# Attention's products a head at a time in halves of TensorE's rows, state and outputs in two banks

## The chip, the core and the metric

The program runs on one core of one Trainium2 chip. The metric is the device time in microseconds (us) of one execution; the median of several runs counts. Engines are named as in the profile: PE is TensorE, PEld its weight loads, DVE VectorE, ACT ScalarE, POOL GpSimd, SP SyncE. SBUF is the on-chip memory, PSUM the eight banks into which PE writes and from which DVE and ACT read.

## The reference

Three blocks follow each other; the change touches the first. Attention (4 batches, 8 heads, 768 positions, head size 48) is a recurrence with a 48x48 state per head:

```
k_n = k / (norm(k) + 1e-06)
for t in range(768):
    y[t] = q[t] @ state
    state += beta[t] * outer(k_n[t], v[t] - k_n[t] @ state)
```

Then `x = y` as [4, 768, 384] goes through a Fourier mix (a DFT over positions and channels, its real part added), a layer norm and a two-layer MLP of width 1536, and last through a gated block with a mix over positions.

## The kernel before

Attention is done in chunks of 64 positions: 12 chunks a batch, 48 in all, ordered so that the four batches run with a lag of four chunks (`SEQ`). A chunk holds 8 heads as 4 pairs (`HP = 4`): head 0 of a pair lies in partitions 0 to 63, head 1 in 64 to 127. For each chunk the recurrence becomes a 64x64 triangular system, which DVE solves for eight chunks at a time (`solve`, L308 and L313 are its products and sums; 1/8 of a solve is dealt to each step), and a few matrix products on PE, all fp32. An fp32 product is two passes, so four products show as x8.

To keep the two heads of a pair apart, a product before the change takes both in one 128-row pass with zeros in the blocks where the heads would mix:

- `stage_b`: TT (block diagonal, 128x128) times keys and values (128x96), into bank Y. ACT copies each half to WU at columns shifted by head, so that the zeros of WU stand where the other head's columns are (L409, two copies of 64x384).
- `stage_c`, not for a batch's first chunk: WU (112 columns) with the masked products (112 columns) into bank Y; DVE subtracts from qt and leaves cw (L421).
- `stage_d`: for each pair gak (112 columns: 64 of outputs, 48 of the state's change) with WU's values (96 columns), plus cw with the state Sb (the second only when the batch has a state), into one tile pd of bank Y, outputs in partitions 0 to 63, state in 64 to 111. ACT copies the state to the two diagonal blocks of Sb (L446) and the outputs to x (L450). In the last chunk of a batch there is no new state.
- At a batch's seventh chunk (`HALF`) one extra row (L439, xr L441) is taken from the state.

The loop over steps t from -3 to 47 writes the order out by hand: `values(t+2)` (ACT scales values by norms, L397, from chunk 29 on partly DVE), part of the solve on DVE, `stage_d(t)`, `stage_c(t+1)`, `stage_a(t+20)` for the later chunks (t from 4 to 27; L221, 112x128 with zero blocks; it stays), `stage_b(t+2)`, and at odd steps `merge`, which puts the solved 32x32 blocks together in small products (L373, L375) and fills TT (L380; `diag`, L361). `chain` holds every engine to the order in which its instructions were written. Stages A of the first chunks (`pairs0` L186, and L219) already take a head at a time, 48 rows and 64 columns each.

From t = 37 on, steps also take pieces of the DFT of finished batches (L603 to L682) and conversions of MLP weights (L712 to L725). Attention's end runs into the MLP's first products (L829) at about 277 us; from 288 us on PE runs the MLP and the gated block.

PSUM: during attention the banks are shared out as X = 4, Y = 3, Z = 1; pb, pc and pd of stages B, C and D take the banks of Y, each waiting for the release of the one it takes.

Of the kernel before, what the change touches and what calls it, by code (L numbers as in the profile page):

```python
# [7 lines left out]
F32 = mybir.dt.float32  # L8
# [8 lines left out]
B, H, S, D = 4, 8, 768, 48  # L17
# [3 lines left out]
C = 64  # L21
NC = S // C
HP = H // 2
# [42 lines left out]
class Kernel:  # L66
# [51 lines left out]
    def attention(self, cp, pg, pe, p, x, filler, after_solves):  # L118
        nc, a, load = self.nc, self.a, self.load
# [9 lines left out]
        TT = [cp.tile([128, 8, 128], F32, name=f"TT{i}") for i in range(NTT)]  # L129

        WU = [cp.tile([128, HP, 256], F32, name=f"WU{i}") for i in range(NWU)]
        Sb = [cp.tile([112, HP, 96], F32, name=f"Sb{i}") for i in range(B)]
        gas, Tts, st, kqs, qts, preps, seen_a = {}, {}, {}, {}, {}, {}, [0]


# [216 lines left out]
        lo, up = qs[::2], qs[1::2]  # L352


        light = lambda t: t >= 8 * NB - 11

        def diag(g8):

            o = (g8 % 4) * 8
            for us in up:  # L360
                (nc.vector.tensor_copy if light(2 * g8 - 3) else nc.scalar.copy)(out=TT[g8 % NTT][us, :, us], in_=Tts[g8 // 4][us, o : o + 8])  # L361

        def merge(g8, first, second):

            z0, z1 = zz[:, g8 % 2 * 256 : g8 % 2 * 256 + 256].rearrange("p (g n) -> p g n", g=8), zz.rearrange("p (g n) -> p g n", g=8)
            T0, o0 = (Tts[g8 // 4] if first else None), (g8 % 4) * 8
            T1, o1 = (Tts[(g8 - 1) // 4] if second else None), ((g8 - 1) % 4) * 8
            tt = TT[(g8 - 1) % NTT]
            for g in range(8):
                for h in range(2):  # L370
                    if first:
                        ga = gas[g8 * 2 + g // 4][:, g % 4]
                        nc.tensor.matmul(z0[lo[h], g], lhsT=ga[up[h], C : C + 32], rhs=T0[up[h], o0 + g], start=True, stop=True)  # L373
                    if second:
                        nc.tensor.matmul(z1[up[h], g], lhsT=T1[lo[h], o1 + g], rhs=ZS[(g8 - 1) % 2][lo[h], g], start=True, stop=True)  # L375
            if first:
                nc.scalar.mul(ZS[g8 % 2][:96, :, 32:], z0[:96], -1.0)
            if second:
                for h in range(2):
                    nc.scalar.copy(out=tt[lo[h], :, 64 * h : 64 * h + 64], in_=z1[up[h]])  # L380


        def load_kv(bc):
# [15 lines left out]
        def stage_b(bc):  # L399
            kv = gas[bc][:, :, C:]  # L400
            tt, o = TT[(bc // 2) % NTT], (bc % 2) * 4
            pb = self.bank("pb", [128, HP, 2, D])
            for hp in range(HP):
                nc.tensor.matmul(pb[:, hp].rearrange("p t d -> p (t d)"), lhsT=tt[:, o + hp], rhs=kv[:, hp], start=True, stop=True)  # L404
            wu = WU[bc % NWU]
            for h in range(2):
                hs, w = slice(64 * h, 64 * h + 64), 112 - 16 * h
                o_ = wu[hs, :, 64 * h : 64 * h + 2 * w].rearrange("p h (t d) -> p h t d", t=2)[:, :, :, :D]
                nc.scalar.copy(out=o_, in_=pb[hs])  # L409
            st[bc] = [wu[:, :, :112], wu[:, :, 112:208], None]  # L410

        def stage_c(bc):
            qt = qts.pop(bc)
            if SEQ[bc][1] == 0:
                return
            w = st[bc][0]
            cw = p.tile([112, HP, 112], F32, name="cw", bufs=2)
            pc = self.bank("pc", [112, HP, 112])
            for hp in range(HP):
                nc.tensor.matmul(pc[:, hp], lhsT=w[:, hp], rhs=gas[bc][:, hp, : C + D], start=True, stop=True)  # L420
            nc.vector.tensor_sub(cw, qt, pc)  # L421
            st[bc][2] = cw

        def stage_d(bc):
            b, c = SEQ[bc]
            ak = gas[bc][:, :, : C + D]
            w, u, cw = st.pop(bc)
            sb = Sb[b]

            m = 112 if c < NC - 1 else C  # L430
            pd = self.bank("pd", [112, HP, 96])
            for hp in range(HP):
                nc.tensor.matmul(pd[:m, hp], lhsT=ak[:, hp, :m], rhs=u[:, hp], start=True, stop=(c == 0))  # L433
                if c > 0:
                    nc.tensor.matmul(pd[:m, hp], lhsT=cw[:, hp, :m], rhs=sb[:, hp], start=False, stop=True)  # L435
            if c == HALF:
                px = self.bank("pb", [128, HP, 2, D])
                for hp in range(HP):
                    nc.tensor.matmul(px[:1, hp], lhsT=qx[:, b, hp : hp + 1], rhs=sb[:, hp], start=True, stop=True)  # L439
                xr = p.tile([1, DM], F32, name="xr", bufs=2)  # L440
                nc.scalar.copy(out=xr, in_=px[:1].rearrange("p h t d -> p (h t d)"))  # L441
                st["x", b] = xr
            if c < NC - 1:
                for h in range(2):
                    hs, cs = slice(64 * h, 64 * h + 48), slice(48 * h, 48 * h + 48)
# [39 lines left out]
        def busy(n, cols):  # L485
# [33 lines left out]
        for t in range(T0, NBC):  # L519
            j, i = divmod(t + 11, 8)  # L520
# [16 lines left out]
            if t >= 0:  # L537
                stage_d(t)
                if SEQ[t][1] == NC - 1:
                    fill.extend(filler(SEQ[t][0]))  # L540
            new = t % 8 == 5 and t + 3 < NBC
            if new:

                merge((t + 3) // 2, True, False)
                load_kv(t + 3)
                load_kv(t + 4)
                diag((t + 3) // 2)
            if 0 <= t + 1 < NBC:
                stage_c(t + 1)
# [799 lines left out]
```

## Time and profile before

| | us |
|---|---|
| median of 3 runs | 855.77 (855.62 to 856.37) |
| the profiled execution's own time | 856.33 |
| its span, first to last instruction | 854.5 |
| PE busy | 829.6 |
| DVE busy | 623.3 |
| ACT busy | 436.0 |

The span is what the profile's rows lie in; the execution's time has 1.8 us around it. Busy time is the union of an engine's instructions. Matmuls are pipelined and their ends modelled: a pass shows some 0.26 us although the next starts 0.1 us later, so the time that a group of passes takes is read from one group's start to the next one's.

### The profile page before, as it was taken

The numbers are of one execution on the slowest core, as the hardware profiler recorded it, in microseconds if no ns is written. First come the engines' busy times: TensorE is split into PE (matmuls) and PEld (weight loads), VectorE is DVE, ScalarE is ACT, GpSimd is POOL, SyncE is SP. The second block draws the span as 40 slices with busy tenths as digits, with TensorE's granted clock in tenths as the row PEclk, the third lists the DMA queues.
The fourth block names the chain that finished last, engine by engine and source line by source line (L and its number), as shares of the span: only waits on it lengthen the run. The fifth ranks groups of instructions, "written<-read, shape, count | busy, mean of one in ns | idle before, by whom it ended". The sixth has DMA issues, their size and how long they took to land.

```text
span 854.5 us, 18425 instructions
## 1 busy us (share of the span) xinstructions
PE 829.6 (97%) x7117; PEld 803.3 (94%) x7117; DVE 623.3 (73%) x1852; ACT 436.0 (51%) x1054; POOL 7.5 (1%) x29
## 2 busy tenths in 40 slices
PE   7879999999999999999999999999999999999998
PEld 7769999999998999899999999999999899899998
DVE  6989999998969897783654891526688377486563
ACT  2669888788876644232224451223472362543632
POOL 2000000000000000000000000000000000000000
PEclk8869999999999999999999999999999999999999
DMA  9365565556450600001022411122101201101101
GB/s 224 84 178 142 169 187 168 162 160 179 133 145 20 240 1 1 1 1 28 2 71 79 130 31 27 35 59 57 37 1 46 67 9 46 58 18 57 38 1 56
DMA packets 57929, 67.21 MB, mean 79 GB/s; under 512 B 31857, under 2 KB 48978, under 8 KB 57842
## 3 DMA queue, kind: packets, MB, share of 16 engines
q1 hardware_dynamic: 57698, 65.89, 26.8%
q8 instruction: 56, 0.92, 0.5%
q14 instruction: 31, 0.25, 0.1%
q10 hardware_dynamic: 144, 0.15, 0.1%
HBM read 53.62 MB, written 4.72 MB: 68 GB/s over the span
## 4 chain that ended last, share of the span: by engine, by line
PE 87%; DVE 9%; ACT 3%; issue 1%; POOL 0%; DVEq 0%; ACTq 0%; POOLq 0%
PE bankX L829 17%; PE bankY L842 15%; PE bankX L1027 10%; PE bankX L1007 6%; PE bankX L975 6%; PE bankY L1055 5%; PE bankY L433 4%; PE bankY L435 4%; PE bankY L420 4%; PE bankY L404 4%; PE bankX L221 2%; PE bankZ L375 2%; PE bankV L842 2%; PE bankX L642 2%; DVE tm L308 1%; DVE Ts L313 1%
## 5 line engine op out<-in xcount | busy, mean ns | idle before, releaser
L842 PE MATMUL bankY<-w,hx 128*128 128x384 f32 x756 | 147.2, 337 | 0.0
L829 PE MATMUL bankX<-uh,w 128*128 128x384 f32 x504 | 137.7, 340 | 0.7 <-DVE ul L751 0.7
L842 PEld LDWEIGHTS bankY<-w,hx 128*128 128x128 f32 x756 | 132.4, 188 | 0.5 <-issue 0.3
L834 DVE SCALAR_TENSOR_TENSOR hx<-bankX,hx 128x384 fp32r<-128x384 f32 x84 | 46.2, 551 | 76.1 <-ACT hx L833 73.6
L833 ACT ACTIVATE hx<-bankX 128x384 fp32r<-128x384 f32 x84 | 41.2, 490 | 111.9 <-PE bankX L829 107.3
L829 PEld LDWEIGHTS bankX<-uh,w 128*128 128x128 f32 x504 | 92.1, 188 | 1.3 <-DVE ul L751 0.9
L1027 PE MATMUL bankX<-w,A 128*128 128x384 f32 x504 | 88.8, 334 | 0.0
L1027 PEld LDWEIGHTS bankX<-w,A 128*128 128x128 f32 x504 | 87.6, 188 | 0.0
L829 PE MATMUL bankX<-ul,w 128*128 128x384 f32 x252 | 85.1, 338 | 0.0
L433 PE MATMUL bankY<-WU,gak 128*112 128x96 f32 (+1 forms) x384 | 70.2, 271 | 0.7 <-ACT x L450 0.7
L435 PE MATMUL bankY<-Sb,cw 112*112 112x96 f32 (+1 forms) x352 | 64.2, 265 | 3.3 <-DVE cw L421 3.1
L313 DVE TENSOR_TENSOR Ts<-Ts,tm 128x110 f32<-128x110 f32 (+26 forms) x264 | 58.9, 259 | 0.9
L308 DVE TENSOR_TENSOR tm<-Ts 128x110 f32<-128x110 f32 (+26 forms) x264 | 58.5, 258 | 0.4
L404 PE MATMUL bankY<-gak,TT 128*128 128x96 f32 x384 | 52.1, 281 | 4.1 <-ACT gak L397 3.6
L409 ACT COPY WU<-bankY 64x384 f32<-64x384 f32 x96 | 45.4, 473 | 20.5 <-PE bankY L404 18.9
L433 PEld LDWEIGHTS bankY<-WU,gak 128*112 128x112 f32 (+1 forms) x384 | 52.3, 178 | 3.7 <-ACT x L450 1.0
L404 PEld LDWEIGHTS bankY<-gak,TT 128*128 128x128 f32 x384 | 48.7, 199 | 4.9 <-ACT gak L397 4.1
L435 PEld LDWEIGHTS bankY<-Sb,cw 112*112 112x112 f32 (+1 forms) x352 | 48.4, 176 | 4.7 <-issue 2.5
L1007 PE MATMUL bankX<-xh,s 128*128 128x384 f32 x192 | 50.0, 338 | 0.0
L1016 ACT CAST u<-hx 128x384 fp32r<-128x384 f32 x32 | 15.8, 514 | 66.6 <-DVE hx L1014 66.6
L829 PEld LDWEIGHTS bankX<-ul,w 128*128 128x128 f32 x252 | 47.3, 188 | 0.0
L975 PE MATMUL bankX<-s,xh 128*128 128x512 f32 x144 | 45.9, 395 | 0.0
(217 smaller groups left out, 1675.8 us busy)
## 6 DMA issues: line engine op xcount, KB each, us to landing
kq<-in_kq_dram SPq DMA_DIRECT2D x24, 448.0 KB, 4.0
qt<-in_qt_dram SPq DMA_DIRECT2D x48, 196.0 KB, 3.6
gak<-in_kv_dram SPq DMA_DIRECT2D x48, 192.0 KB, 3.9
w<-in_w_dram SPq DMA_DIRECT2D x24, 384.0 KB, 5.6
out_dram<-x SPq DMA_DIRECT2D x24, 192.0 KB, 1.9
kq<-in_kc_dram SPq DMA_DIRECT2D x8, 448.0 KB, 10.8
x<-x SPq DMA_DIRECT2D x96, 36.0 KB, 1.9
s<-in_wi_dram SPq DMA_DIRECT2D x6, 512.0 KB, 4.2
```

The source lines that it names most:

```text
L308: nc.vector.tensor_tensor(out=tm, in0=T[:, r, k : k + 1].to_broadcast(sh), in1=T[:, k : k + 1, :k].to_broadcast(sh), op=MUL)
L313: nc.vector.tensor_add(o, o, tm)
L404: nc.tensor.matmul(pb[:, hp].rearrange("p t d -> p (t d)"), lhsT=tt[:, o + hp], rhs=kv[:, hp], start=True, stop=True)
L409: nc.scalar.copy(out=o_, in_=pb[hs])
L433: nc.tensor.matmul(pd[:m, hp], lhsT=ak[:, hp, :m], rhs=u[:, hp], start=True, stop=(c == 0))
L435: nc.tensor.matmul(pd[:m, hp], lhsT=cw[:, hp, :m], rhs=sb[:, hp], start=False, stop=True)
L829: nc.tensor.matmul(ph, lhsT=w1[f][i][:, c * 128 : c * 128 + 128], rhs=cur[k][:, c], start=(c + j == 0), stop=(c == 2 and j == 2))
L834: nc.vector.scalar_tensor_tensor(out=hl, in0=ph, scalar=0.0, in1=hh.bitcast(F32), op0=MAX, op1=SUB)
L842: nc.tensor.matmul(acc[t], lhsT=hx[i][:, t * 128 : t * 128 + 128], rhs=w2[e][k], start=(e == 0 and j == 0), stop=(e == 11 and j == 2),)
L975: nc.tensor.matmul(pv, lhsT=xT[t][i][:, c, kk * 128 : kk * 128 + 128], rhs=wi[2 * c + 1][k], start=(c + j == 0), stop=(c == 2 and j == 2))
L1007: nc.tensor.matmul(pu, lhsT=wi[2 * c][i][:, f * 128 : f * 128 + 128], rhs=xT[hf][k][:, c], start=(c + j == 0), stop=(c == 2 and j == 2))
L1027: nc.tensor.matmul(acc, lhsT=A[:, m, o, i, kk], rhs=Bo[name, kk][:, k], start=(kk + j == 0), stop=(kk == 2 and j == 2))
```

## The change

Every product of stages B, C and D is taken for one head at a time, with that head's 64 (or 48) rows as the only rows of the pass, and the zero blocks go: TT is 64 columns wide, WU 96, Sb 48. `hs` are the two heads' halves of 64 partitions, `ds` their first 48.

- `stage_b`: 8 products of 64 rows, 64 columns, 96 streamed; one copy of 128x384 to WU.
- `stage_c`: 8 products of 64 rows, 64 columns (48 that count), 112 streamed.
- `stage_d`: state and outputs become products of their own, in two tiles `ps` and `po`, each in its own bank of Y: for each pair, each source (values, state) and each head one product for the state (48 columns) and one for the outputs (64), 48 streamed. Head 0 writes its state to partitions 0 to 47 and its outputs to 64 to 127; head 1 its state to 64 to 111 and its outputs to 0 to 63. The outputs are copied by two instructions of 64x192.
- The extra row: 8 products into partitions 0 and 64, two copies.
- The fills of WU and Sb with zeros go; the fill of TT, whose first tile also feeds the warming products at the start, is half as long.

```
-            for hp in range(HP):
-                nc.tensor.matmul(pb[:, hp].rearrange(...), lhsT=tt[:, o + hp], rhs=kv[:, hp], start=True, stop=True)
+            for hp in range(HP):
+                for h in hs:
+                    nc.tensor.matmul(pb[h, hp].rearrange(...), lhsT=tt[h, o + hp], rhs=kv[h, hp], start=True, stop=True)
...
-            for h in range(2):
-                ...
-                nc.scalar.copy(out=o_, in_=pb[hs])
+            nc.scalar.copy(out=wu, in_=pb.rearrange("p h t d -> p h (t d)"))
...
-                nc.tensor.matmul(pc[:, hp], lhsT=w[:, hp], rhs=gas[bc][:, hp, : C + D], start=True, stop=True)
+                for h in hs:
+                    nc.tensor.matmul(pc[h, hp], lhsT=w[h, hp, :C], rhs=gas[bc][h, hp, : C + D], start=True, stop=True)
...
-            pd = self.bank("pd", [112, HP, 96])
+            po, ps = self.bank("pd", [128, HP, D]), None
+            if c < NC - 1:
+                ps = self.bank("pd", [128, HP, D])
             for hp in range(HP):
-                nc.tensor.matmul(pd[:m, hp], lhsT=ak[:, hp, :m], rhs=u[:, hp], start=True, stop=(c == 0))
-                if c > 0:
-                    nc.tensor.matmul(pd[:m, hp], lhsT=cw[:, hp, :m], rhs=sb[:, hp], start=False, stop=True)
+                for last in (False, True)[: 1 + (c > 0)]:
+                    end = last == (c > 0)
+                    for i, h in enumerate(hs):
+                        k, u = (cw[ds[i], hp], sb[ds[i], hp]) if last else (ak[h, hp], wu[h, hp, D:])
+                        if ps is not None:
+                            nc.tensor.matmul(ps[ds[i], hp], lhsT=k[:, C:], rhs=u, start=not last, stop=end)
+                        nc.tensor.matmul(po[hs[1 - i], hp], lhsT=k[:, :C], rhs=u, start=not last, stop=end)
...
+                for i in range(2):
+                    for hp in range(HP):
+                        nc.tensor.matmul(px[C * i : C * i + 1, hp, i], lhsT=qx[ds[i], b, hp : hp + 1], rhs=sb[ds[i], hp], start=True, stop=True)
+                    nc.scalar.copy(out=xr.rearrange(...)[:, :, i], in_=px[C * i : C * i + 1, :, i])
...
-                    nc.scalar.copy(out=sb[hs, :, cs], in_=pd[64:112, :, cs])
+                for d in ds:
+                    nc.scalar.copy(out=sb[d], in_=ps[d])
...
-            nc.scalar.copy(out=x[b][js, tl], in_=pd[:64].rearrange("p h e -> p (h e)"))
+            for i in range(2):
+                nc.scalar.copy(out=x[b][js, tl].rearrange(...)[:, :, i], in_=po[hs[1 - i]])
...
-        for t in WU + Sb:
-            nc.gpsimd.memset(t, 0.0)
```

## Rows read from the trace of the kernel before

**Rows 1.** The page's part 1: busy us of each engine, share of the span, instructions

```profile
PE 829.6 (97%) x7117; PEld 803.3 (94%) x7117; DVE 623.3 (73%) x1852; ACT 436.0 (51%) x1054; POOL 7.5 (1%) x29
```

**Rows 2.** Windows: stretch; length, then busy PE, PEld, DVE, ACT, POOL (count), granted clock, DMA

```profile
12.00:38.00 26.00, 20.18 (x345) 19.04 (x341) 25.36 (x127) 15.07 (x53) 0.15 (x1) 0.87 0.57 143
38.00:74.00 36.00, 27.94 (x398) 26.32 (x399) 33.21 (x139) 24.81 (x68) 0.82 (x6) 0.72 0.55 142
74.00:190.00 116.00, 115.04 (x1695) 110.39 (x1695) 113.20 (x448) 101.10 (x281) 1.14 (x8) 1.00 0.61 172
190.00:240.00 50.00, 49.45 (x811) 47.16 (x809) 46.47 (x138) 41.16 (x104) 0.15 (x1) 1.00 0.57 160
240.00:288.00 48.00, 46.22 (x476) 43.17 (x474) 37.88 (x98) 33.96 (x79) 0.00 (x0) 1.00 0.38 125
```

**Rows 3.** Timeline of DVE, two stretches: start, us from first start to last end

```profile
27.64 0.46 DVE L308 TENSOR_TENSOR tm<-Ts 128x119 f32<-128x119 f32 x2
...
96.41 0.47 DVE L308 TENSOR_TENSOR tm<-Ts 128x119 f32<-128x119 f32 x2
```

**Rows 4.** Waits from 74 to 240 us: total us, times, longest

```profile
DVE cw L421 <- PE bankY L420: 2.2, 6, 0.6
...
DVE gak L227 <- PE bankX L221: 0.9, 4, 0.3
```

**Rows 5.** Timeline of PE, one step: start, us to the last end, passes (x)

```profile
97.03 0.36 PE L433 MATMUL bankY<-WU,gak 128*112 128x96 f32 x2
...
98.60 0.96 PE L420 MATMUL bankY<-gak,WU 128*112 128x112 f32 x8
99.41 1.07 PE L221 MATMUL bankX<-kq 112*128 112x128 f32 x8
100.31 1.03 PE L404 MATMUL bankY<-gak,TT 128*128 128x96 f32 x8
101.27 0.21 PE L373 MATMUL bankZ<-Tc,gak 32*32 32x32 f32 x1
```

**Rows 6.** Timeline of PEld and PE: loads in halves; products of the last chunk

```profile
8.12 1.36 PEld L186 LDWEIGHTS bankX<-gak 48*64 48x64 f32 x44
...
22.31 1.11 PEld L219 LDWEIGHTS bankX<-kq 48*64 48x64 f32 x19
...
211.31 0.33 PE L435 MATMUL bankY<-Sb,cw 112*64 112x96 f32 x2
211.48 0.33 PE L433 MATMUL bankY<-WU,gak 128*64 128x96 f32 x2
```

**Rows 7.** Timeline of PE around the extra row of a batch

```profile
203.76 0.36 PE L435 MATMUL bankY<-Sb,cw 112*112 112x96 f32 x2
204.05 0.82 PE L439 MATMUL bankY<-Sb,qx 112*1 112x96 f32 x8
204.80 1.04 PE L420 MATMUL bankY<-gak,WU 128*112 128x112 f32 x8
205.67 0.60 PE L404 MATMUL bankY<-gak,TT 128*128 128x96 f32 x4
```

**Rows 8.** Timeline of DVE, late in attention; in brackets the wait before

```profile
254.40 0.56 DVE L725 TENSOR_TENSOR w<-cvd,w 128x384 fp32r<-128x384 f32 x1 [4.54 <-ACT w L724]
```

**Rows 9.** Timeline of ACT in one step

```profile
134.02 0.64 ACT L446 COPY Sb<-bankY 48x192 f32<-48x192 f32 x2
134.67 0.47 ACT L450 COPY x<-bankY 64x384 f32<-64x384 f32 x1
...
136.01 0.97 ACT L409 COPY WU<-bankY 64x384 f32<-64x384 f32 x2
```

**Rows 10.** Timeline of PE, ACT and DVE at another extra row

```profile
94.38 1.04 PE L420 MATMUL bankY<-gak,WU 128*112 128x112 f32 x8
94.65 0.47 ACT L441 COPY xr<-bankY 1x384 f32<-1x384 f32 x1
...
95.88 0.61 DVE L421 TENSOR_TENSOR cw<-qt,bankY 112x448 f32<-112x448 f32 x1
```

More of the change, by code (lines that the diff above doesn't have):

```diff
@@ L128, in attention @@
         NTT = NWU = 2
-        TT = [cp.tile([128, 8, 128], F32, name=f"TT{i}") for i in range(NTT)]
-        WU = [cp.tile([128, HP, 256], F32, name=f"WU{i}") for i in range(NWU)]
-        Sb = [cp.tile([112, HP, 96], F32, name=f"Sb{i}") for i in range(B)]
+        TT = [cp.tile([128, 8, C], F32, name=f"TT{i}") for i in range(NTT)]
+        WU = [cp.tile([128, HP, 2 * D], F32, name=f"WU{i}") for i in range(NWU)]
+        Sb = [cp.tile([112, HP, D], F32, name=f"Sb{i}") for i in range(B)]
+        hs, ds = (slice(0, C), slice(C, 2 * C)), (slice(0, D), slice(C, C + D))
         gas, Tts, st, kqs, qts, preps, seen_a = {}, {}, {}, {}, {}, {}, [0]
@@ L360, in diag @@
             for us in up:
-                (nc.vector.tensor_copy if light(2 * g8 - 3) else nc.scalar.copy)(out=TT[g8 % NTT][us, :, us], in_=Tts[g8 // 4][us, o : o + 8])
+                (nc.vector.tensor_copy if light(2 * g8 - 3) else nc.scalar.copy)(out=TT[g8 % NTT][us, :, 32:], in_=Tts[g8 // 4][us, o : o + 8])
         def merge(g8, first, second):
@@ L379, in merge @@
                 for h in range(2):
-                    nc.scalar.copy(out=tt[lo[h], :, 64 * h : 64 * h + 64], in_=z1[up[h]])
+                    nc.scalar.copy(out=tt[lo[h]], in_=z1[up[h]])
         def load_kv(bc):
@@ L403, in stage_b @@
             for hp in range(HP):
-                nc.tensor.matmul(pb[:, hp].rearrange("p t d -> p (t d)"), lhsT=tt[:, o + hp], rhs=kv[:, hp], start=True, stop=True)
+                for h in hs:
+                    nc.tensor.matmul(pb[h, hp].rearrange("p t d -> p (t d)"), lhsT=tt[h, o + hp], rhs=kv[h, hp], start=True, stop=True)
             wu = WU[bc % NWU]
-            for h in range(2):
-                hs, w = slice(64 * h, 64 * h + 64), 112 - 16 * h
-                o_ = wu[hs, :, 64 * h : 64 * h + 2 * w].rearrange("p h (t d) -> p h t d", t=2)[:, :, :, :D]
-                nc.scalar.copy(out=o_, in_=pb[hs])
-            st[bc] = [wu[:, :, :112], wu[:, :, 112:208], None]
+            nc.scalar.copy(out=wu, in_=pb.rearrange("p h t d -> p h (t d)"))
+            st[bc] = [wu, None]
         def stage_c(bc):
@@ L417, in stage_c @@
             cw = p.tile([112, HP, 112], F32, name="cw", bufs=2)
-            pc = self.bank("pc", [112, HP, 112])
+            pc = self.bank("pc", [128, HP, 112])
             for hp in range(HP):
-                nc.tensor.matmul(pc[:, hp], lhsT=w[:, hp], rhs=gas[bc][:, hp, : C + D], start=True, stop=True)
-            nc.vector.tensor_sub(cw, qt, pc)
-            st[bc][2] = cw
+                for h in hs:
+                    nc.tensor.matmul(pc[h, hp], lhsT=w[h, hp, :C], rhs=gas[bc][h, hp, : C + D], start=True, stop=True)
+            nc.vector.tensor_sub(cw, qt, pc[:112])
+            st[bc][1] = cw
         def stage_d(bc):
@@ L426, in stage_d @@
             ak = gas[bc][:, :, : C + D]
-            w, u, cw = st.pop(bc)
+            wu, cw = st.pop(bc)
             sb = Sb[b]
-            m = 112 if c < NC - 1 else C
-            pd = self.bank("pd", [112, HP, 96])
+            po, ps = self.bank("pd", [128, HP, D]), None
+            if c < NC - 1:
+                ps = self.bank("pd", [128, HP, D])
             for hp in range(HP):
-                nc.tensor.matmul(pd[:m, hp], lhsT=ak[:, hp, :m], rhs=u[:, hp], start=True, stop=(c == 0))
-                if c > 0:
-                    nc.tensor.matmul(pd[:m, hp], lhsT=cw[:, hp, :m], rhs=sb[:, hp], start=False, stop=True)
+                for last in (False, True)[: 1 + (c > 0)]:
[5 more added lines that the diff above has]
+                        nc.tensor.matmul(po[hs[1 - i], hp], lhsT=k[:, :C], rhs=u, start=not last, stop=end)
             if c == HALF:
                 px = self.bank("pb", [128, HP, 2, D])
-                for hp in range(HP):
-                    nc.tensor.matmul(px[:1, hp], lhsT=qx[:, b, hp : hp + 1], rhs=sb[:, hp], start=True, stop=True)
                 xr = p.tile([1, DM], F32, name="xr", bufs=2)
-                nc.scalar.copy(out=xr, in_=px[:1].rearrange("p h t d -> p (h t d)"))
+                for i in range(2):
+                    for hp in range(HP):
+                        nc.tensor.matmul(px[C * i : C * i + 1, hp, i], lhsT=qx[ds[i], b, hp : hp + 1], rhs=sb[ds[i], hp], start=True, stop=True)
+                    nc.scalar.copy(out=xr.rearrange("p (h t d) -> p h t d", h=HP, t=2)[:, :, i], in_=px[C * i : C * i + 1, :, i])
                 st["x", b] = xr
             if c < NC - 1:
-                for h in range(2):
-                    hs, cs = slice(64 * h, 64 * h + 48), slice(48 * h, 48 * h + 48)
-                    nc.scalar.copy(out=sb[hs, :, cs], in_=pd[64:112, :, cs])
+                for d in ds:
+                    nc.scalar.copy(out=sb[d], in_=ps[d])
             cc = c if c < HALF else NC - 1 - c
@@ L449, in stage_d @@
             tl = cc // 2 + (0 if c < HALF else 3)
-            nc.scalar.copy(out=x[b][js, tl], in_=pd[:64].rearrange("p h e -> p (h e)"))
+            for i in range(2):
+                nc.scalar.copy(out=x[b][js, tl].rearrange("p (h t d) -> p h t d", h=HP, t=2)[:, :, i], in_=po[hs[1 - i]])
             if c == NC - 1:
```

## Prediction

> **What bounds the kernel now.** I read the page's busy line first [rows 1]: PE is busy 97% of the span, but its ends are modelled, so the line does not say that a shorter product shortens the kernel. The change lies in attention, which runs to about 288 us, so the second view is the windows by stage [rows 2]. From 74 to 190 us PE is busy 115.04 us of 116 and DVE 113.20; from 190 to 240 us it is 49.45 and 46.47 of 50; only from 240 to 288 us does DVE fall behind, 37.88 of 48 against 46.22. Two engines look full in the loop; one only keeps pace. The third view settles which: DVE's own rows [rows 3]. At 27.64 us, while nothing but the solve of the first block runs, two solver products of 119 columns take 0.46 us. At 96.41 us, in the loop, the same two take 0.47. DVE works at its own pace in the loop, with hardly a hole between instructions. The view of waits agrees: from 74 to 240 us DVE waits for PE's products 2.2 and 0.9 us [rows 4], 3.1 us in 166. So up to 240 us the kernel is bound by DVE, which the change does not touch (the subtraction at L421 keeps its 112x448 shape), and a faster PE can give back some 3 us there, no more. Behind 288 us nothing changes; what attention gains or loses moves the end by as much.
>
> **PE, by products.** An fp32 product is two passes in the rows (x8 for four). Now, with the full array [rows 5]: the 16 passes of stage D (L433, L435) take 98.60 - 97.03 = 1.57 us, 98 ns each with 112 columns of weights; stage C (L420) 0.81; stage A (L221, 128 columns) 0.90, 112 ns each; stage B (L404), also 128 columns, the same 0.90 (0.96 here, with a change of shape behind it, below). With 64 columns of weights and 96 streamed a pass takes 0.17/2 = 85 ns (L435 to L433 at 211 us [rows 6]). In halves of the rows the trace has two kinds: 44 loads of 64 columns within 1.36 us (L186, 64 streamed), at most 31 ns each, and 19 within 1.11 us (L219, 128 streamed), at most 58 [rows 6]. Two halves therefore run beside each other: a pair costs about what one full pass of that shape costs.
> B: 16 passes at 85/2 = 0.68, saving 0.22. C: 16 with 112 streamed, between 85/2 and 58, say 49: 0.79, saving 0.02. D grows from 16 to 64 passes, with 48 or 64 columns of weights and 48 streamed, over all four quarters of the array. The halves in the trace differ in rows and in columns; two passes in the same rows and other columns it does not show. If the quarters run side by side, each has 16 passes at no more than 62 ns (two of L186's 31): 0.99, at best 0.93; D saves 0.6. If only rows overlap, each half has 16 passes at 62 and 16 at some 3/4 of that (48 columns): 1.74, at best 1.6; D loses up to 0.17. No overlap at all is excluded [rows 6]. I take the first, since any two successive blocks of D differ in quarter, which is what L186's passes do, and keep the second for the range.
> [...]
> **A cost that the diff does not name** is the change between array shapes. The row of a batch's extra product shows one [rows 7]: L435 to L439 (one column of weights) 0.29 us instead of 0.20, L439 to L420 0.75 instead of its own eight passes at 80 ns (its 0.82 us less the 0.26 that a single pass shows, over seven), and then L420 0.87 instead of 0.81. That is 0.09 + 0.11 + 0.06, about 0.25 us a round trip. Stage A keeps its full-array products at steps 4 to 27 and now stands between C and B in halves: 24 round trips that were not there. The filler products of the DFT (four steps from 240 us) get one each. The last chunk of a batch, now 64 columns wide in all its products [rows 6], loses its own.
> Sum for PE, per step with A: -0.60 - 0.22 - 0.02 + 0.25 = -0.59 with quarters, +0.18 (up to) with rows alone; without A -0.84 and -0.07.
>
> **What of it reaches the end.** 74 to 240 us: of the 3.1 us of waits I count 2.5 back; the rest of the PE time is hidden by DVE. 240 to 259 us: three steps in which PE sets the pace and DVE stands 4.54 us at once [rows 8]. Two of them gain 0.84 less a round trip and the wait for a bank (below), 0.35 each; the third has a last chunk, whose D is 16 passes of 85 ns and now only outputs, 8 passes of 62 a quarter, 0.9 less. Together 1.6. From 259 us DVE is busy again and I count nothing.
> **ACT**: stage B's two copies (0.97 us the pair [rows 9]) become one of the same 384 columns, 0.48 less; the output copy of 0.47 becomes two of 192 columns, 0.64 by the pair of state copies: +0.17. Net 0.3 less a step on an engine with room (101.10 of 116 [rows 2]): nothing by itself. Should ACT have no room, it is what frees the banks.
> **Banks.** A step took three banks of Y (D, C, B) out of three; now it takes four. B(t+2) can start only when the first of outputs, state and C's bank is free, and that is the state's, after its two copies, 0.64 us behind D's end. C and A (1.7 us) cover it to step 27. Without A, C alone (0.79) does not quite: 0.1 to 0.3 us of PE in some 20 steps. DVE hides most in the loop; I take 0.5 us (bounds 0 and 3).
> **The extra row of each batch** (L439, four times) takes a fifth tile. C must then wait until xr's two copies are done. At 94 us [rows 10] the copy starts at 94.65, behind the values, and takes 0.47; C starts already at 94.38. Two copies of half the length, bounded by 0.47 each and taken as 0.3, put C at 95.25, its end and the subtraction at about 96.2 instead of 95.88: 0.35 us of DVE, more where DVE already waits; three in the loop, 1.5 us (bounds 0.5 and 3).
> **Start.** Fills of WU and Sb go (POOL, off the path: they follow TT's) and TT's halve. TT's fill gates the warming products, so the first real ones may come some tenths earlier: 0.2 us.
> Sum: -0.2 - 2.5 - 1.6 + 0.5 + 1.5 = -2.3 us. The profiled execution took 856.33 us with a span of 854.5 and 1.8 around it: 854.0. It lies 0.56 above the median of the runs shown, so against the median it is 853.5.
>
> **Rivals.**
> *Rows overlap, columns do not* (slower). PE then needs up to 0.18 us more in each of 24 steps with A, 3 to 4 us in all, and since it is now level with DVE [rows 2] it becomes the bound. Without A its saving is 0.07, so that the waits for a bank show: 2.5 us. With the extra rows' 1.5, and 0.5 back between 240 and 259 us, +6: 862. For it: nothing in the trace shows the other. Against it: the passes that do overlap are as short as these. [...]
> *The bank binds* (slower). If B is given the outputs' bank instead of the state's, ACT's chain from values over state and output copies stands ahead of every B. That is 0.64 us later in each step, which A covers no longer once D is short, since ACT's copies, not PE, then set the step. It decides from the point where ACT's work and its waits for B exceed the 4.8 us that a step takes (116 us over 24 steps [rows 2]). At 0.15 us in 24 steps and 0.5 in 10, with 1.5 for the extra rows and 1.6 won back, +8: 864.
> *DVE hides all of it*: what comes back in the loop is less than 1.5 us, the extra rows eat it: 854.5 to 857. This is the upper part of my own case and shares its chance.
> [...]
>
> **How the numbers follow.** A measurement here tells about 0.2% (1.7 us) from no change. Quarters side by side with DVE as bound: 0.55, its own range 850 to 857; over half of it lies beyond 0.2% faster. Rows alone 0.25, the bank 0.10, the earlier clock 0.10. Faster 0.30 + 0.09 = 0.39; same 0.22 from the first and 0.06 from the edges of the others; slower 0.03 + 0.22 + 0.08 = 0.33. The range leaves out a tenth on the slow side and less on the fast one: 848 to 864.
>
> **What would show it.** Right: in the profile after, D of 64 passes in 0.9 to 1.05 us, B in 0.7, A followed and preceded by 0.1 us more; DVE's busy time from 74 to 240 us unchanged and its waits for L420 below 1 us except at the extra rows; the whole loop shorter by under 3 us. Wrong: D at 1.6 us or more; B waiting for ACT's copies of state or outputs for microseconds in sum; a granted clock below 1.00 inside the loop, as PE now has holes there.

## The result, and the profile after

The changed kernel takes 861.9 us (median of 5 runs, 859.28 to 865.49); the kernel before took 856.37 beside it. The ratio is 1.0064, 95% interval 1.0034 to 1.0093: slower by 0.64%, where 853.5 us and faster were forecast. The profiled execution of the changed kernel took 860.85 us, with a span of 859.1.

The page's part 1 (as [rows 1]) and, of part 3, the queue that brings instructions (packets, MB, share):

```profile
PE 803.4 (94%) x9965; PEld 764.4 (89%) x9965; DVE 623.9 (73%) x1852; ACT 419.1 (49%) x1058; POOL 3.5 (0%) x23
...
q8 instruction: 78, 1.28, 0.6%
```

PE is 26 us less busy, DVE does the same work, and yet the span is 4.6 us longer. PE runs 9965 passes instead of 7117, each with a load. The instruction queue had 56 packets before: 22 more packets for 2 x 2848 more instructions, 259 to a packet of 16 KB.

The windows of attention, in the columns of [rows 2], and the last three stretches of half clock within it:

```profile
74.00:190.00 116.00, 102.89 (x3042) 90.84 (x3040) 110.86 (x444) 90.66 (x276) 0.47 (x3) 0.99 0.62 171
190.00:240.00 50.00, 40.79 (x1534) 35.81 (x1528) 46.00 (x137) 36.80 (x104) 0.16 (x1) 1.00 0.57 164
240.00:288.00 48.00, 41.49 (x920) 37.96 (x921) 35.47 (x92) 29.14 (x75) 0.00 (x0) 0.93 0.29 86
...
95.30:98.60 3.30, 3.30 (x77) 3.08 (x79) 3.20 (x16) 1.25 (x4) 0.00 (x0) 0.50 0.42 130
242.10:245.40 3.30, 3.30 (x86) 3.16 (x87) 1.48 (x4) 3.18 (x8) 0.00 (x0) 0.50 0.43 100
276.20:279.50 3.30, 3.30 (x75) 3.02 (x66) 2.62 (x9) 1.16 (x4) 0.00 (x0) 0.50 0.00 0
```

From 74 to 190 us PE fell from 115.04 to 102.89 us, as the shorter products should make it; but DVE, which should have become the only bound, fell too, from 113.20 to 110.86. It waits more. Three times the granted clock drops to half (0.50 in these rows, for 3.4 us each), which it never did behind 63 us before. The waits from 74 to 240 us, PE's and DVE's (as [rows 4]; "issue" is a wait for nothing that the profile shows):

```profile
PE bankY L405 <- ACT Sb L451: 6.9, 11, 1.0
PE bankY L440 <- DVE cw L421: 4.3, 8, 0.8
PE bankY L420 <- issue: 2.0, 2, 1.0
PE bankY L446 <- ACT xr L447: 1.9, 3, 1.0
PE bankY L420 <- ACT xr L447: 1.2, 3, 0.4
PE bankZ L373 <- issue: 1.2, 3, 0.7
...
DVE cw L421 <- PE bankY L420: 4.3, 5, 1.4
DVE gak L227 <- PE bankX L221: 1.6, 4, 0.5
```

DVE's waits for PE went from 3.1 to 5.9 us instead of towards 0.6. PE's waits for cw (4.3 us) are what a PE ahead of DVE must have. Beside them three new waits stand in its list: stage B for the state's copies, the extra row and C for xr's copies, and "issue". When they cost something is seen at the subtraction L421, of which each chunk but a batch's first has one. Its start in the kernel before (us), and how much later (+) or earlier it came in the changed kernel and in four of the runs below:

| start before | changed | row in X | + four banks | fewer instructions | B, C alone |
|---|---|---|---|---|---|
| 58.15 | -0.84 | -1.09 | -0.83 | -0.96 | -1.43 |
| 90.25 | -2.09 | -2.32 | -2.08 | +1.08 | -0.48 |
| 95.88, extra row | -1.14 | -2.32 | -2.08 | +1.08 | -0.44 |
| 115.91 | -0.03 | -2.64 | -2.41 | +0.86 | +1.05 |
| 148.77, extra row | +0.54 | -2.99 | -2.22 | +0.49 | +1.73 |
| 169.16 | +0.47 | -3.34 | -2.29 | +0.24 | +2.22 |
| 174.12 | +1.33 | -1.98 | -1.47 | +0.24 | +2.59 |
| 201.70 | +0.23 | -1.51 | -1.00 | +1.12 | +2.79 |
| 205.87, extra row | +1.13 | -1.65 | -0.99 | +0.69 | +2.67 |
| 210.32 | +1.26 | -0.39 | +1.24 | +0.79 | +2.56 |
| 238.28 | +0.96 | -0.70 | +0.98 | +0.50 | +2.32 |
| 242.39 | +2.83 | -0.71 | +0.98 | +0.50 | +2.50 |
| 248.99, extra row | +3.68 | +0.81 | +1.33 | +1.40 | +2.46 |
| 258.98 | +3.46 | +0.57 | +0.41 | +1.31 | +2.16 |
| 274.84 | +4.13 | +0.64 | +0.93 | +1.38 | +2.38 |

The changed kernel comes 2.1 us early into the loop and loses 6.2 us in it, in jumps: at the four extra rows (0.95, 0.5, 0.9, 0.85), behind the clock's fall at 95 us (1.1), at 174, and at 242.

### The profile page after: what moved, and what is told of

It reads as the page before. It is cut to its first block, busy times and chain, and to the rows that moved or that the text cites. A ratio compares the mean times of both kernels' runs of the same rounds, so it can differ in the third digit from the quotient of the medians.

```text
span 859.1 us, 24110 instructions
## 1 busy us (share of the span) xinstructions
PE 803.4 (94%) x9965; PEld 764.4 (89%) x9965; DVE 623.9 (73%) x1852; ACT 419.1 (49%) x1058; POOL 3.5 (0%) x23
## 4 chain that ended last, share of the span: by engine, by line
PE 77%; DVE 15%; ACT 5%; issue 2%; POOL 0%; DVEq 0%; ACTq 0%; POOLq 0%
PE bankX L832 17%; PE bankY L845 15%; PE bankX L1030 10%; PE bankX L1010 6%; PE bankX L978 6%; PE bankY L1058 5%; DVE tm L308 3%; DVE Ts L313 3%; PE bankY L420 3%; PE bankY L405 2%; PE bankV L845 2%; PE bankX L221 2%; PE bankX L645 2%; PE bankZ L375 2%; PE bankY L440 1%
## 5 line engine op out<-in xcount | busy, mean ns | idle before, releaser
L405 PE MATMUL bankY<-gak,TT 64*64 64x96 f32 x768 | 44.6, 257 | 17.3 <-ACT Sb L451 10.6
L440 PE MATMUL bankY<-WU,gak 64*64 64x48 f32 x768 | 51.3, 231 | 6.8 <-DVE cw L421 5.1
L405 PEld LDWEIGHTS bankY<-gak,TT 64*64 64x64 f32 x768 | 35.8, 139 | 24.5 <-ACT Sb L451 15.0
L420 PE MATMUL bankY<-gak,WU 64*64 64x112 f32 x704 | 47.8, 271 | 4.3 <-issue 2.0
L440 PE MATMUL bankY<-Sb,cw 48*64 48x48 f32 x704 | 47.0, 226 | 1.6 <-issue 0.8
L440 PEld LDWEIGHTS bankY<-WU,gak 64*64 64x64 f32 x768 | 40.5, 141 | 8.7 <-DVE cw L421 6.1
L439 PE MATMUL bankY<-WU,gak 64*48 64x48 f32 x704 | 44.1, 218 | 0.0
```

The lines of the kernel that those rows point to most:

```text
L405: nc.tensor.matmul(pb[h, hp].rearrange("p t d -> p (t d)"), lhsT=tt[h, o + hp], rhs=kv[h, hp], start=True, stop=True)
L420: nc.tensor.matmul(pc[h, hp], lhsT=w[h, hp, :C], rhs=gas[bc][h, hp, : C + D], start=True, stop=True)
L439: nc.tensor.matmul(ps[ds[i], hp], lhsT=k[:, C:], rhs=u, start=not last, stop=end)
L440: nc.tensor.matmul(po[hs[1 - i], hp], lhsT=k[:, :C], rhs=u, start=not last, stop=end)
```

## The experiments

Eighteen kernels tell four causes apart that these jumps suggest: the extra row, the state's bank, the clock, and PE's waits for nothing. All results, with the packets of the instruction queue, PE's "issue" waits from 66 to 290 us, and the median over the runs of the mean granted clock (before: 56, none, 0.984):

| run | us | ratio to before (95%) | packets | issue, us | clock |
|---|---|---|---|---|---|
| changed | 861.9 | 1.0064 (1.0034 to 1.0093) | 78 | 6.7 | 0.978 |
| row in X | 858.8 | 1.0023 (1.0010 to 1.0037) | 78 | 5.8 | 0.981 |
| four banks | 860.3 | 1.0039 (1.0020 to 1.0057) | 78 | 10.3 | 0.982 |
| row in X, four banks | 856.7 | 0.9997 (0.9985 to 1.0010) | 78 | 11.4 | 0.982 |
| row in X, fewer instructions | 853.3 | 0.9959 (0.9944 to 0.9975) | 69 | 0.9 | 0.979 |
| row in X, 128 more at the start | 859.4 | 1.0030 (1.0016 to 1.0044) | 79 | 8.9 | 0.978 |
| row in X, product in the hole | 859.0 | 1.0034 (1.0020 to 1.0048) | 79 | 5.4 | 0.984 |
| row in X, A in halves | 859.9 | 1.0030 (1.0015 to 1.0045) | 80 | 10.0 | 0.978 |
| row in X, merge first | 858.1 | 1.0007 (0.9997 to 1.0017) | 78 | 8.0 | 0.983 |
| row in X, four banks, merge first | 856.7 | 1.0004 (0.9991 to 1.0018) | 78 | 10.2 | 0.981 |
| changed, merge first | 861.7 | 1.0047 (1.0030 to 1.0064) | 78 | 8.8 | 0.978 |
| before, merge first | 860.2 | 1.0044 (1.0032 to 1.0056) | 56 | none | 0.984 |
| D in row halves | 874.4 | 1.0221 (1.0191 to 1.0251) | 68 | none | 0.977 |
| B, C alone | 858.6 | 1.0033 (1.0018 to 1.0047) | 62 | 0.2 | 0.984 |
| D alone, row in X | 860.5 | 1.0035 (1.0023 to 1.0047) | 72 | 2.7 | 0.982 |
| the same, four banks | 858.7 | 1.0020 (1.0005 to 1.0034) | 73 | 2.9 | 0.980 |
| before, early fill | 857.0 | 1.0004 (0.9986 to 1.0023) | 56 | none | 0.984 |
| the same, first five chunks | 856.8 | 0.9998 (0.9989 to 1.0006) | 58 | none | 0.984 |
| the same, first and last | 858.2 | 1.0022 (1.0011 to 1.0033) | 63 | 3.8 | 0.983 |

**The extra row in a bank of X.**

```
-                px = self.bank("pb", [128, HP, 2, D])
+                px = self.bank("pf", [128, HP, 2, D])
...
+                for i in range(2):
                     nc.scalar.copy(out=xr..., in_=px[C * i : C * i + 1, :, i])
```

> The changed kernel with the extra row's tile in a bank of X instead of Y, and with all eight of its products ahead of its two copies. If the fifth tile and the wait between its halves cost what the starts of the subtraction L421 show (some 0.9, 0.5, 0.9 and 0.8 us at its four places), the kernel gets 2 to 3 us shorter than the changed one (858.5 to 860), and the waits for xr's copies are gone. Rival, clock and supply of instructions set the time: under 1 us, since what PE gains at these places DVE or the next hole takes back.

0.41% of the 0.64% is gone, some 3 us. The intervals of this pair just overlap; two other pairs that differ by the same edit, with four banks and with the merge first (both below), give 0.42% and 0.40% with intervals apart. Three of the four jumps at the extra rows (95.88, 148.77, 205.87) are none now. At the fourth, 248.99, 1.5 us are still lost, with a wait of B for the state's copies (1.15 us) just ahead of it, so the changed kernel's jump there is not shown to be the extra row's. In the changed kernel the first of these places reads, PE and ACT (in brackets the wait before):

```profile
91.34 0.50 PE L446 MATMUL bankY<-Sb,qx 48*1 48x48 f32 x8
92.81 0.50 PE L446 MATMUL bankY<-Sb,qx 48*1 48x48 f32 x8 [0.97 <-ACT xr L447]
93.71 0.98 PE L420 MATMUL bankY<-gak,WU 64*64 64x112 f32 x16 [0.40 <-ACT xr L447]
...
91.41 1.01 ACT L397 ACTIVATE gak<-gak,n_all 128x48 f32<-128x48 f32 x4
92.45 0.31 ACT L447 COPY xr<-bankY 1x192 f32<-1x192 f32 x1
93.34 0.31 ACT L447 COPY xr<-bankY 1x192 f32<-1x192 f32 x1 [0.59 <-PE bankY L446]
```

PE's second eight passes wait for the copy of the first eight, which is queued behind the values on ACT; then C waits for the second copy. The prediction had only the last of the two waits. The run takes away both, and how the 3 us divide between them is open.

**Four banks for B, C and D.** `self.psum(dict(X=3, Y=4, Z=1))` for attention; first alone, later with the row in X.

> The changed kernel with four banks for B, C and D instead of three (X gets three instead of four) during attention. If the bank binds, B's wait for the state's copies (10 us of PE in 14 places) goes and the kernel comes down by 3 us or more, to 858 or less. If DVE hides that wait, it stays within 1 us of the changed kernel (861 to 862.5), with B's waits gone from the list all the same; PE's holes then lie elsewhere, and the falls of the granted clock stay.

> The changed kernel with the extra row in a bank of X and four banks for B, C and D (X gets three). If the bank costs some 1 to 1.6 us on top of the extra row, as the run with four banks alone suggests, 857 to 858 (the same as the kernel before); the waits for instructions stay at 6 to 10 us. If DVE hides the bank's wait here too, 858.5 to 859.

B's wait for the state's copies left the list. Alone, the bank gave 0.25%, which the intervals don't separate; on top of the row in X it gave 0.26%, 858.8 to 856.7, level with the kernel before, with intervals that just touch. What the profiles show of it lies from 240 us on: from 238.28 to 258.98 the kernel with the row in X loses 1.3 us, with two such waits of B (1.15 and 0.46 us); with four banks as well it gains 0.6. Up to 240 us DVE hides it: in the changed kernel three such waits (1.0, 0.56 and 0.38 us) lie between the subtractions at 115.91 (-0.03) and 144.74 (+0.02), which they do not move. The whole gain stands on the medians: in the profiles, from 90.25 to 238.28, the kernel with the row in X and four banks loses 1.4 us more than that with three, and the two end level (+0.93 and +0.64).

**How D is cut.** One product of 112 columns for a head's state and outputs, each head in its own bank:

```
-                        if ps is not None:
-                            nc.tensor.matmul(ps[ds[i], hp], lhsT=k[:, C:], rhs=u, ...)
-                        nc.tensor.matmul(po[hs[1 - i], hp], lhsT=k[:, :C], rhs=u, ...)
+                        nc.tensor.matmul(pd[i][:m, hp], lhsT=k[:, :m], rhs=u, ...)
```

> The changed kernel with D in halves of the rows alone: one product of 112 columns for state and outputs of a head, a bank for each head, half as many passes in D (32 instead of 64). If quarters are what makes D short, D goes back from 0.9 to some 1.4 to 1.6 us. If PE's stalls without a releaser come from the number of its instructions, they go (from some 6 us to under 1), and the packets of the instruction queue fall from 78 to some 66. If the granted clock falls because PE has holes, it now stays at 1.00 from 63 us on, and the kernel takes 856 to 858. Rival, the clock has nothing to do with it and the longer D costs: 862 or more.

18 us slower than before. First D and the next stages in the changed kernel, then the run's D (rows left out are the like):

```profile
106.62 0.27 PE L440 MATMUL bankY<-WU,gak 64*64 64x48 f32 x2
...
107.48 0.29 PE L440 MATMUL bankY<-Sb,cw 48*64 48x48 f32 x4
107.96 0.98 PE L420 MATMUL bankY<-gak,WU 64*64 64x112 f32 x16 [0.20 <-ACT WU L407]
108.88 1.16 PE L221 MATMUL bankX<-kq 112*128 112x128 f32 x8
109.97 0.88 PE L405 MATMUL bankY<-gak,TT 64*64 64x96 f32 x16
```

```profile
106.77 0.36 PE L436 MATMUL bankY<-Sb,cw 48*112 48x48 f32 x4
106.96 0.36 PE L436 MATMUL bankY<-WU,gak 64*112 64x48 f32 x4
107.16 0.36 PE L436 MATMUL bankY<-Sb,cw 48*112 48x48 f32 x4
```

In quarters, 64 passes start within 0.92 us. In halves of the rows, four passes with 112 columns of weights take 0.195 us, 97 ns a pair, just what one full pass took before [rows 5]: two halves run beside each other, but a pass of 112 columns lasted as long with 64 and 48 rows as with 128 and 112. Quarters are what shortens D: to C's start it takes 1.34 us in them (106.62 to 107.96) and 1.70 in this run (106.14 to 107.84). PE is busy 113.33 of 116 us again in this run, "issue" is none, and the four extra rows cost 1.6 to 2.6 us each, 8 of the 18; the rest no run takes apart. The clock did not stay at 1.00, as it should have if only long holes made it fall: it fell at 154.1 and 215.6 us, each time at an extra row, whose two holes are 0.4 us each.

**B and C alone, D alone.** B and C in halves with D, copies and zero blocks of before; then D in quarters with B and C of before, with three banks and with four.

> Stages B and C in halves as changed, stage D, the copies, the zero blocks of WU and Sb and the extra row as before. B then costs 0.68 and C 0.75 us, with two changes of shape more a step (0.25 each round trip), so PE is as full as before. If the loss lies in D's banks, the extra row and PE's holes, this takes what the kernel before takes: 855.5 to 857, with the granted clock at 1.00 in the loop. If the changes of shape cost DVE time, 858 or more.

> Stage D in quarters with its two banks as changed; B and C as before (full array, zero blocks of TT and WU kept, B's two copies), the extra row in a bank of X, the first tile's fill split so that the warming products start as early as in the changed kernel. Three changes of shape fewer a step than B and C in halves would make them: A then takes 0.80 us from first to last pass again, C 0.70, and D stays at 0.92. If the changes of shape and the number of instructions cost the changed kernel its gain, this takes 853 to 856. If the waits for a bank and the falls of the granted clock do, 857 to 860, as PE has the same holes.

> Stage D alone in quarters (B and C as before), the extra row in a bank of X, four banks for B, C and D. Waits for instructions some 3 us, as in the run of D alone (2.7), no wait for the state's bank. If that wait cost D alone its 3 us, 856 to 857.5; if ACT's copies (two more a step than the changed kernel needs) do, 859 to 861.

Each part alone is slower than before. A step of the run with B and C:

```profile
107.32 0.43 PE L435 MATMUL bankY<-WU,gak 128*112 128x96 f32 x2
...
109.06 0.98 PE L422 MATMUL bankY<-gak,WU 64*64 64x112 f32 x16
109.97 1.16 PE L221 MATMUL bankX<-kq 112*128 112x128 f32 x8
111.06 0.88 PE L405 MATMUL bankY<-gak,TT 64*64 64x96 f32 x16
111.87 0.24 PE L375 MATMUL bankZ<-ZS,Tc 32*32 32x64 f32 x2
```

D takes 1.74 us to C's start, C 0.91, A 1.09, B 0.81: 4.55. In [rows 5] the same four took 1.57, 0.81, 0.90 and 0.96, together 4.24. B's own passes are shorter, but every stage now changes the array's shape. PE has no slack there (115.56 of 116 us busy), and the subtractions fall back from -0.48 to +2.8 by 201.70. D alone keeps 2.7 us of "issue" and has one more copy of ACT a step than the changed kernel; C then waits for B's copies (7.2 us with four banks), and the expected 853 to 856 did not come.

**PE's waits for nothing.** Two such holes, within stage C of the run with the row in X, and what the DMA view of that run shows of queue 8 from 168.8 to 170.3 us; from 170.3 to 171.7 us it has no packet:

```profile
171.70 0.41 PE L420 MATMUL bankY<-gak,WU 64*64 64x112 f32 x3 [1.38 <-issue]
...
209.10 0.69 PE L420 MATMUL bankY<-gak,WU 64*64 64x112 f32 x10 [1.37 <-issue]
```

```profile
q8 instruction: 1, 0.02, 5.9%
```

In the trace that packet ends at 170.23, and the product goes on 1.47 us behind it. Of the six holes over 0.9 us of this kind from 165 to 242 us in the changed kernel and this run, each ends 1.40 to 1.47 us behind a packet's end; the 38 of all runs end 1.2 to 1.7 us behind one, while packets come some 4.7 us apart in the changed kernel. If they are waits for instructions, a shift of the packets' boundaries must move them:

```
+        wb = self.bank("pd", [32, 1])
+        for i in range(32):
+            nc.tensor.matmul(wb, lhsT=warm[:32, :32], rhs=warm[:32, :1], start=True, stop=True)
         busy(CF["last"], 512)
```

> The kernel of the extra row in a bank of X (858.8), with 32 tiny products (32x32 weights, one column, read by nothing; 128 instructions of PE with their loads) ahead of the chunks' loop, at some 50 us. They move the boundaries of the instruction queue's packets by half a packet (one is 16 KB; 22 more came with 5,696 more instructions, 259 each) and nothing else in the loop. If PE's stalls without a releaser are waits for such packets, they move to other places than C at 171.7 and 209.1 us, M at 238.9 and B at 201.2, and each still ends 1.2 to 1.6 us after a packet's end; the time may be up to 3 us less or 2 more. Rival, these products themselves wait for something that the profile doesn't show: the same places, the same lengths.

They moved. The holes at 171 and 209 us are gone, and others stand elsewhere (near 201 and 240 us there still are some, the longest 1.55 us, but within D instead of B and the merge):

```profile
102.22 0.56 PE L420 MATMUL bankY<-gak,WU 64*64 64x112 f32 x7
105.05 1.01 PE L420 MATMUL bankY<-gak,WU 64*64 64x112 f32 x6 [2.27 <-issue]
...
205.19 0.20 PE L440 MATMUL bankY<-WU,gak 64*64 64x48 f32 x1 [1.01 <-issue]
```

The first ends 1.46 us behind a packet's end (103.59), the second 1.42. Nothing else in the loop had changed. Then the price, by taking instructions out without making PE's step shorter. The kernel computes less: head 1's products of a pair in D give way to two of 192 columns, whose results mean nothing.

```
-                    for i, h in enumerate(hs):
+                    h = hs[0]
...
+            k, u = (cw[ds[1], 0], sb[ds[1]]) if c > 0 else (ak[h, 0], wu[h, :, D:])
+            if ps is not None:
+                nc.tensor.matmul(ps[ds[1]], lhsT=k[:, C:], rhs=u, start=True, stop=True)
+            nc.tensor.matmul(po[hs[0]], lhsT=k[:, :C], rhs=u, start=True, stop=True)
```

> The kernel of the extra row in a bank of X, with less of stage D: head 1's products of a pair (32 of the 64 passes) are replaced by two products of 192 columns (4 passes), so that head 1's state and outputs are not the reference's; head 0's 32 passes, 16 in each of their two quarters, stay, and so should D's duration (0.85 to 0.95 us) and all waits for DVE and ACT. The instruction queue's packets fall from 78 to some 68. If PE's waits for instructions cost what the late C at 174 and 210 us and the late steps at 240 us cost, the stalls without a releaser fall below 1 us and the time by 2 to 3 us, to 856 to 857. Rival, DVE's pace hides them or the waits for banks take their place: 858 to 859.

0.9959 against 1.0023: 5.5 us on the medians. From 90.25 to 274.84 its subtractions lose 0.3 us, those of its base 3.0, those of the changed kernel 6.2. So the profiles show 2.7 of the 5.5 us: the profiled execution of this run was its slowest, 857.74 us, with a longer stretch of half clock ahead of the loop, and DVE still waits 3.3 us for PE in it from 74 to 240 us. The medians gain more than the 2 to 3 us expected, and why is open. D is no shorter (its first pass at 107.52, C's at 108.86: 1.34 us, as in the changed kernel), B waits for the state's copies as before, and from 74 to 240 us "issue" is gone:

```profile
PE bankY L405 <- ACT Sb L457: 6.0, 14, 0.8
PE bankY L440 <- DVE cw L421: 3.6, 8, 0.7
PE bankY L405 <- ACT n L140: 0.8, 1, 0.8
PE bankY L405 <- ACT x L462: 0.7, 1, 0.7
PE bankY L440 <- ACT x L462: 0.4, 1, 0.4
```

More instructions go the other way, with A in halves too (`pa[q, hp]` from each half of `kq`, 16 passes for 8):

> The kernel of the extra row in a bank of X with stage A in halves as well (16 passes of 64 columns of weights, 128 streamed, instead of 8), so that no stage of a step changes the array's shape. A's way from C's last pass to B's first goes from 1.27 us to some 1.1; three packets of instructions come on top. If the changes of shape cost the kernel time, 1 us less or more (857.8); if DVE hides PE's time and the supply of instructions sets the losses, the same or up to 1.5 us more (858.5 to 860.5).

Beside the merge's small products no change of shape is left in a step: from C's first pass to B's it takes 1.69 us (105.69 to 107.38), where the changed kernel takes 2.01. "Issue" is 10.0 us in 14 places, and the time is no better than that of its base.

**Is it how closely they follow?** The merge's 64 passes and D's 64 stand back to back at odd steps. With the merge ahead of B (the call moved up four lines):

> The kernel of the extra row in a bank of X (858.8), with the merge ahead of stage B at odd steps instead of behind it: the same instructions, the merge in the hole in which PE waits for the state's copies, and B's products between the merge and D. If the waits for instructions come from bursts that follow each other too closely, they get fewer (from some 7 us to 3 or less) and the time falls by 1.5 to 3 us, to 856 to 857.5. If the number alone decides, the waits stay and lie elsewhere: 858 to 859.5.

> The changed kernel (861.9) with only the merge ahead of stage B at odd steps, the extra row left in its fifth tile. If bursts are the cause, 1.5 to 3 us less, 859 to 860.5, and still the extra row's 0.5 to 0.9 us at each of its places; if the number alone decides, 861 to 863.

> The kernel before, with only the merge ahead of stage B at odd steps. PE has no holes there and no waits for instructions, and DVE sets the pace: within 0.5 us of the kernel before. If the order itself gains or costs (through the shorter or longer way from the merge to the next stage B), it shows here: 1 us or more either way.

> As the run before it, with the merge ahead of stage B at odd steps. With four banks there is no hole before B that the merge could fill, so the order gains nothing: the same within 1 us, or 1 to 2 us more, as the order alone costs the kernel before 3 us.

"Issue" did not get less (8.0 and 8.8 us); over half of it now stands at the merge's own passes. So the number counts, as far as this order can tell. The sum of "issue" is not its price, though: with the same 78 packets it is 5.8 to 11.4 us, most where B no longer waits for its bank, and the fastest version of the whole change (856.7) has the 11.4. The first run gained 0.7 us on its base, with intervals that overlap; it fills the hole before B, whose wait goes from 12.7 to 1.2 us. Where there is no hole, the order costs 0.4% or gives nothing.

**The clock.** One product a step for the hole before B, read by nothing:

```
+            if 2 <= bc < 40:
+                n = 192 if 6 <= bc < 30 else 256
+                nc.tensor.matmul(self.bank("pf", [128, n]), lhsT=mk[:, :128], rhs=mk[:, :n], start=True, stop=True)
```

> The kernel of the extra row in a bank of X (858.8), with one product (128x128 weights, 192 or 256 columns of the masks, read by nothing) ahead of each stage B of chunks 2 to 39, where PE waits for the state's copies. If the granted clock falls because PE stands in holes, there are fewer falls from 74 us on (in the profile none), and the time comes down by up to 2 us, to 857. Rival, the holes that matter are others (cw before D's second half, the stalls without a releaser): falls as often as without it, time the same or up to 3 us more, since PE gets 0.4 us more a step.

The clock is back at the 0.984 of the kernel before (0.981 without these products), and the time is not better. So here the falls came at least in part from these holes, and filling them with work gains nothing. One fall is left in the profile, at 272.5 us, behind a hole of 1.62 us that got no product.

**Start and ends.**

> The kernel before, with only the start as in the changed kernel: the part of the first tile that the warming products read (128x512) is filled ahead of its rest. If the early gain of the changed kernel (0.84 us at the first subtraction L421) comes from the start of the warming products, 0.5 to 1 us less than before: 855.5. If it comes from shorter products under the lower clock, no difference.

> The kernel before with the early fill, and B, C and D in halves and quarters, state and outputs in two banks, only for the first five chunks (to some 76 us, where PE has the lower clock and each chunk waits for the one before); from the sixth on as before, with one bank for D. If the gain of the changed kernel lies in these steps (1.2 us between the first and the fourth subtraction) and its loss in the loop behind them, 1 to 1.5 us less than the early fill alone: 855 to 856. Rival, the clock's steps at the start decide: within 0.5 us of the early fill alone (857.0).

> As the run with the first five chunks, and also for chunks 37 to 47 (from some 238 us), where DVE stands still and PE sets the pace. If shorter products help where PE sets the pace, 1 to 1.6 us less again: 854 to 855. Rival, at that place the fourth bank of a step and the supply of instructions take it back: the same as with the first five alone, or up to 1.5 us more.

The early start is worth nothing on the medians, nor are shorter products for the first five chunks, though both show in the subtractions (-2.7 and -1.5 us by the fourth). In the profiles of both, the granted clock falls to half for 3.4 us at 360 to 365 us, far behind attention; in that of before it does not. With the last chunks too, 1.4 us are lost: 3.8 us of "issue" and a fall of the clock at 242.6 us. No version here is faster than the kernel before and computes all of it.

## Why the prediction was wrong

**PE's prices: right.** From first to last start D takes 0.92 us (forecast 0.93 to 0.99), B 0.64 (0.68), C 0.73 (0.79). *Rows overlap, columns do not*, with 1.6 us or more for D, is refuted; that the 861.9 measured is its 862 is luck (its own terms add up to 6.5 to 7.5 us rather than 6). A round trip of shapes around A was taken as 0.25 us and costs 0.30: from C's first pass to B's 2.01 us (107.96 to 109.97), where it was 1.71 (98.60 to 100.31 in [rows 5]).

**"The rest of the PE time is hidden by DVE", the 2.5 us back from 74 to 240 us: this step failed.** The sum had PE's passes by their durations alone and nothing that brings them, no term for 2848 more passes at all. With 40% more PE instructions (78 packets of them instead of 56) PE runs out of them: 6.7 us of waits in ten places, some inside C, on which DVE waits. With them nearly gone (0.9 us, 69 packets), 5.5 us come back on the medians and 2.7 in the profiled loop. Nothing in the trace of before shows such a wait of PE in the loop; its 56 packets were there to be read.

**The extra row: mechanism half right, size too small.** 1.5 us for three places in the loop, bounds 0.5 to 3; the three jumps in the profile make 2.4, the medians 3.1. The wait between its own halves was missed.

**The bank: 0.5 us, bounds 0 to 3; measured 2.2** on the medians (0.26%). B does wait for the state's copies, as the sum had it. That C and A cover this up to step 27 is wrong: six of these waits, 4.1 us, stand there; but DVE hides them, and what shows lies behind 240 us, which the prediction booked as a gain. *The bank binds* had B wait for the outputs' bank, which it does not.

**"240 to 259 us: -1.6" failed too.** DVE's wait there [rows 8], for a conversion on ACT, was taken as set by PE. It hardly follows PE. With fewer instructions it reads as in the first line; the second is the one wait of PE over 0.6 us in this stretch of the changed kernel:

```profile
255.71 0.56 DVE L734 TENSOR_TENSOR w<-cvd,w 128x384 fp32r<-128x384 f32 x1 [4.44 <-ACT w L733]
...
241.38 0.21 PE L373 MATMUL bankZ<-Tc,gak 32*32 32x32 f32 x1 [1.80 <-issue]
```

4.44 us, where it was 4.54; in the changed kernel it is 4.31, with the row in X and four banks 3.61. On top come, in the changed kernel, this wait for instructions, the clock's fall at 242 us and the extra row's two holes (0.56 and 0.40 us): from 238.28 to 258.98 2.5 us are lost where 1.6 were to be won.

**The clock.** The earlier clock, which has 0.10 of the chances, held in the profile and not on the medians: the granted clock is 1.00 from 61.1 us on up to the fall at 95, before from 62.6, and the subtraction at 90 us comes 2.1 us earlier; no run shows a gain of the whole from it. The falls inside the loop, which the prediction listed as a sign of its being wrong, come behind holes. What they cost apart from the holes is open: the falls at 95, 242 and 276 us stand beside jumps of 1.1, 1.9 and 0.6 us, and each follows on holes of 1.4 to 1.8 us in sum that cost something by themselves.

By the medians the three causes sum to 3.1 + 2.2 + 5.5 = 10.8 us; the changed kernel is 8.4 us above the 853.5 forecast (7.8 counted from the 856.4 of the kernel before beside it). That they hide one another, as one wait covers the next, is likely but not shown, as no run takes all three away; and medians of kernels that spread over 5 us carry an error of a microsecond or so each.

## What to carry to other kernels

Cutting a product into pieces that run beside each other bought time on TensorE here (D to C's start 1.34 us instead of 1.57) and paid in instructions (2848 more passes, 6.7 us of PE's waits): count them per microsecond, beside the packets of the instruction queue that the page already shows. Where another engine sets the pace, a shorter product gains at most that engine's waits (3.1 us here), while every new tile, copy and hole can cost the full price; a tile that is used once a batch, in a ring of three banks and with a wait between its halves, cost as much here as all of DVE's waits in the loop had been worth. And before a wait is booked as a gain, ask which engine ends it, and what that engine is waiting for.

## What was not expected of the hardware

- PE's waits for instructions (read so, as 128 more at the start move them and 0.9 us are left with 69 packets) have no releaser in the profile; the 38 over 0.9 us in these runs end 1.2 to 1.7 us behind the end of a 16 KB packet.
- A pass in a quarter of the array cost 14 ns with all four in use (64 passes start within 0.92 us); one with 112 columns of weights took 97 to 98 ns with 128 rows or with 64, but two of 64 rows ran in that time.
- From 66 us on the granted clock fell to half for 3.4, 6.8 or 10.2 us at a time, mostly behind holes of 0.7 to 3.0 us in PE's work, with D in row halves behind two of 0.4 us at an extra row; and not after every longer hole (one of 1.6 us at 273 us, with the row in X, had none).
